# Memsets between all GpSimd record scatters and first row gathers, one set of head sums moved to VectorE, and the surplus table built in the second expert

## The chip, the cores and the metric

The kernel runs on one core of a Trainium2 chip. The metric is the device time of one execution in microseconds (us). A core has the engines TensorE (PE, with its weight loads shown as PEld), VectorE (DVE), ScalarE (ACT), GpSimd (POOL) and SyncE (SP); SP and POOL issue the DMAs, and each engine works through its own instruction list in order.

## The reference, cut to what matters

```python
def _attn_ref(q, k, v):                      # 8 batches, 8 heads, 576 rows, 64 wide
    k_p = k.reshape(B, H, Sp, 8, D).mean(axis=3)      # keys and values pooled by 8: 72 of them
    v_p = v.reshape(B, H, Sp, 8, D).mean(axis=3)
    attn = softmax(q @ k_p.T / sqrt(D))
    return attn @ v_p

def _moe_ref(x, w_gate, w_noise, noise, w1, w2):      # x: 4608 tokens x 512, 8 experts
    noisy = x @ w_gate + log1p(exp(x @ w_noise)) * noise
    top2 = two largest of noisy per token; top2_w = softmax of the two
    for e in range(8):
        h = relu(x[mask_e] @ w1[e])                   # 512 -> 1024
        out[mask_e] += top2_w * (h @ w2[e])           # 1024 -> 512
```

Attention makes x; a router picks two of eight experts per token; each expert computes only its own tokens.

## The kernel before, in words

**Attention and routing.** Four pairs of batches follow each other, nine chunks of 128 tokens a pair. For each chunk TensorE makes scores, transposed weights and the output; ScalarE takes the exponentials; VectorE takes maxima, divides, and writes `x` (to DRAM) and per-head router sums `lg`. At the end of a pair `route` (a generator that is advanced piece by piece between chunks) adds the eight heads' sums up (lines 512 and 513, the head sums: on GpSimd for the first two pairs, on VectorE for the last two), finds the top two experts, and ranks each token within its expert by TensorE prefix sums. Each token's record (token, weight, where to send the result) is then written to its place in `rec_dram` by an indirect DMA of GpSimd: 18 scatters a pair, 128 records each (`scatter`, line 642). While attention runs, a memset of a spare tile `spacer` (line 649) stands between one scatter and the next; once it is over (`attending[0] = False`), none does.

**What hangs on the scatters.** GpSimd's list is one chain. After the second pair's 18 scatters it loads the first expert's first records (line 692) and gathers their token rows, tiles `xg0` to `xg3` (line 719); then come the third pair's 18 scatters, a load, and `xg4`, `xg5`; then the fourth pair's 18 scatters, the record loads that SP issues, and `xg6` to `xg9`.

**The experts.** Expert 0 is computed in three groups of tiles (0 to 3, 4 and 5, 6 to 9), every other expert in three too. `stage1` multiplies by w1 (line 1031), `stage2` by w2 (line 1142; line 1108 in the last group of an expert). For expert 0 the rows of a group are transposed on TensorE (`rows_of`, line 769) in the middle of the group before: those of the second group between its second and third tile, those of the third group, `xg6` to `xg9`, after the first of the two tiles of the second group's `stage2`. TensorE works in order, so a row tile that is late there holds up everything behind it. All matmuls are in three passes of fp32r pieces; the weights' pieces are made by ScalarE and VectorE (lines 480 and 481).

**The surplus table** (lines 1212 to 1248) lists experts with more tokens than planned, from the final counts `cnt`. It is written last in the code, but the scheduler puts its VectorE instructions where `cnt` is ready, in the first expert's first group, and its two small DMAs on SP there.

Of the kernel before, what the change touches and what calls it, by code (L numbers as in the profile page):

```python
# [8 lines left out]
F32 = mybir.dt.float32  # L9
F32R = mybir.dt.float32r  # L10
BF16 = mybir.dt.bfloat16
I32 = mybir.dt.int32
AF = mybir.ActivationFunctionType
OP = mybir.AluOpType
AX = mybir.AxisListType.X
# [4 lines left out]
def kernel(  # L20
# [12 lines left out]
    nc = tc.nc  # L33
    B, H, S, D = q.shape
    NTOK, DM = out.shape
    E = moe_w_gate.shape[1]
    DF = moe_w1.shape[2]
    P = 128
# [7 lines left out]
    NP = B // 2  # L46
# [4 lines left out]
    CAP = 1216  # L51
    OV_T = -(-(NTOK - CAP) // P)
    ER = CAP + OV_T * P
# [18 lines left out]
    dp = ctx.enter_context(tc.tile_pool(name="scratch", bufs=1, space=bass.MemoryType.DRAM))  # L72
    rp = ctx.enter_context(tc.tile_pool(name="route", bufs=1))
# [3 lines left out]
    rec_dram = dp.tile([E * ER, RW], I32, name="rec_dram")  # L77
# [4 lines left out]
    prow = cp.tile([P, 1], F32, name="prow")  # L82
# [407 lines left out]

    scq = []
    pace = [None]
    tail_rec = [None]
    attending = [True]
    spacer = ap_.tile([P, DM], F32, name="spacer")

    def route(pr, c0, c1, lg, psum):
        n = c1 - c0
# [8 lines left out]
        V = nc.vector  # L507
        L = t(NCH, 2 * E)
        for a, b in ((c0, c1 - 1), (c1 - 1, c1)):
            eng = nc.gpsimd if pr < NP // 2 else V  # L510
            for h in (4, 2):
                eng.tensor_add(lg[:, a:b, :h], lg[:, a:b, :h], lg[:, a:b, h:2 * h])
            eng.tensor_add(L[:, a - c0:b - c0], lg[:, a:b, 0], lg[:, a:b, 1])
            if b < c1:
                yield
                if pr < NP - 1:
                    yield
# [120 lines left out]
        V.tensor_add(word(2), later, tb)  # L638

        def scatter(c, i):  # L640
            def put():
                return nc.gpsimd.indirect_dma_start(  # L642
                    out=rec_dram[:, :],
                    out_offset=bass.IndirectOffsetOnAxis(ap=pos[:, i, c:c + 1], axis=0),
                    in_=rec[:, c, i, :], in_offset=None)

            if attending[0] and tail_rec[0] is not None:
                with tc.issue_after(tail_rec[0].ins), tc.issue_after(pace[0].ins):
                    gap = nc.gpsimd.memset(spacer, 0.0)
                with tc.issue_after(gap.ins):  # L650
                    s = put()
            else:
                s = put()
            tail_rec[0] = s
            tc.declare_no_dep(s.ins, group="rec_scatter", reason="distinct rows")
            if pr >= NP // 2:
                tc.declare_no_dep(s.ins, group="rec_load0", reason="rows of the other half")
            if pr == NP - 1:
                tc.declare_no_dep(s.ins, group="rec_load1", reason="rows of the other pairs")
            tc.add_to_no_dep_group("rec_scatter", s.ins)  # L660
            tc.add_manual_dep(s.ins, pace[0].ins.name,
                              mybir.DependencyInfo(mybir.DependencyClass.Sync, mybir.DependencyReason.DATA),
                              reason="paced")
# [52 lines left out]
    def gather(e, t):  # L716
        xg = wp.tile([P, DM], F32, tag="xg", name=f"xg{e}_{t}", bufs=4)
        if e == 0:
            g = nc.gpsimd.indirect_dma_start(
                out=xg, out_offset=None, in_=x_dram[:XT0 if t < 4 else NTOK, :],  # L720
                in_offset=bass.IndirectOffsetOnAxis(ap=xi[e, t], axis=0))
            if t < 4:
                tc.declare_no_dep(g.ins, group="xw1", reason="rows of the other half")
                tc.add_to_no_dep_group("xg0", g.ins)
        else:
            nr = 2 if t == 9 else 4
            row = pools[0].tile([P, DM], F32, tag="row", name=f"row{e}_{t}", bufs=4)
            turn_of("pool", lambda: nc.gpsimd.indirect_dma_start(  # L728
                out=row[:32 * nr], out_offset=None, in_=x_dram[:, :],
                in_offset=bass.IndirectOffsetOnAxis(ap=xi[e, t][:32 * nr], axis=0)))  # L730
            via = dp.tile([P, DM], F32, tag="via", name=f"via{e}_{t}", bufs=4)
            for r in range(nr):
                turn_of("sp", lambda: nc.sync.dma_start(
                    via.rearrange("(u j) (r c) -> j r u c", u=4, r=4)[:, r],
                    row[32 * r:32 * r + 32].rearrange("j (u c) -> j u c", u=4)))
            back.append(lambda: turn_of("sp", lambda: nc.sync.dma_start(xg[:, :nr * P], via[:, :nr * P])))
        XG[e, t] = xg
# [207 lines left out]
            gens.append(route(pr, 0, 5, lgs[pr], one))  # L945
    due.pop()()
    advance(100, 0)
    attending[0] = False
    ctx2.close()


# [37 lines left out]
    def count(e):  # L989
        rows[e] = nc.values_load(cnti[0:1, e:e + 1], engines=[mybir.EngineType.PE], min_val=0, max_val=NTOK)  # L990
# [179 lines left out]
    def hook1(i, f):  # L1170
        if i == 0 and f == 0:
            with tc.issue_after(s0[0].ins), tc.issue_after(s0[1].ins):
                next(rt, None)
        elif i == 0:
            next(rt, None)
            next(rt, None)
        advance(0, POPS[i][f])
# [10 lines left out]
                nc.gpsimd.drain()  # L1188

    NG = 3  # L1190
    for i, g in enumerate(groups):
        e = g[0]
        if i % NG == 1 and e + 1 < E:
            wgens += [weights(e + 1, 0), weights(e + 1, 1)]
        if joined(g):
            with tc.issue_after(lastmm[0].ins):
                count(e)
        stage1(g, (lambda f: hook1(i, f)) if i < 2 else flush if i == len(groups) - 1 else None)
        if i > 1:
            if i + 1 < len(groups):  # L1200
                with tc.issue_after(HT[g][-1][2].ins):
                    split(groups[i + 1])
        if i % NG:
            wadvance(100)
        if i % NG == NG - 1 and e + 1 < E:
            wgens += [weights(e + 1, 2), weights(e + 1, 3)]
        stage2(g, (lambda t, mm: hook(i, t, mm)) if i < 2 else None,
               groups[i + 2] if 0 < i < len(groups) - 2 else None)


    thr = rp.tile([P, OV_T], F32, name="thr")
    nc.gpsimd.iota(thr, pattern=[[P, OV_T]], base=CAP, channel_multiplier=0,
                   allow_small_or_imprecise_dtypes=True)
    NJ = E
    cj = cnt
    gt = rp.tile([P, E, OV_T], F32, name="gt")
    nc.vector.tensor_tensor(gt, cj.unsqueeze(2).to_broadcast([P, E, OV_T]),
                            thr.unsqueeze(1).to_broadcast([P, E, OV_T]), op=OP.is_gt)
    nt_ = rp.tile([P, NJ], F32, name="nt")
    nc.vector.tensor_reduce(out=nt_, in_=gt, axis=AX, op=OP.add)  # L1220
    cum = rp.tile([P, NJ], F32, name="cum")
    nc.vector.tensor_copy(cum[:, 0:1], nt_[:, 0:1])
    for j in range(1, NJ):
        nc.vector.tensor_add(cum[:, j:j + 1], cum[:, j - 1:j], nt_[:, j:j + 1])
    le = rp.tile([P, NJ], F32, name="le")
    nc.vector.tensor_scalar(le, cum, prow, None, op0=OP.is_le)
    ln_ = rp.tile([P, NJ], F32, name="ln")
    nc.vector.tensor_mul(ln_, le, nt_)
    red = rp.tile([P, 2], F32, name="red")
    nc.vector.tensor_reduce(out=red[:, 0:1], in_=le, axis=AX, op=OP.add)  # L1230
    nc.vector.tensor_reduce(out=red[:, 1:2], in_=ln_, axis=AX, op=OP.add)
    sg = rp.tile([P, 2], F32, name="sg")
    nc.vector.tensor_sub(sg[:, 1:2], prow, red[:, 1:2])
    nc.vector.tensor_scalar(sg[:, 0:1], red[:, 0:1], float(ER), float(CAP), op0=OP.mult, op1=OP.add)
    nc.vector.scalar_tensor_tensor(sg[:, 0:1], sg[:, 1:2], float(P), sg[:, 0:1], op0=OP.mult, op1=OP.add)
    NTAB = 64
    nc.vector.scalar_tensor_tensor(sg[:, 1:2], red[:, 0:1], -float(CAP), sg[:, 0:1], op0=OP.mult, op1=OP.add)
    nc.vector.tensor_single_scalar(sg[:, 1:2], sg[:, 1:2], float(P + (E - 1) * CAP), op=OP.add)
    tab = rp.tile([P, 3], I32, name="tab")
    nc.vector.tensor_copy(tab[:, 2:3], sg[:, 1:2])  # L1240
    nc.vector.tensor_copy(tab[:, 0:1], sg[:, 0:1])
    nc.vector.tensor_copy(tab[:, 1:2], red[:, 0:1])
    tot = rp.tile([P, 1], I32, name="tot")
    nc.vector.tensor_copy(tot, cum[:, NJ - 1:NJ])
    tab_dram = dp.tile([NTAB, 3], I32, name="tab_dram")
    nc.sync.dma_start(tab_dram[:, :], tab[:NTAB])
    tabr = rp.tile([1, 3 * NTAB], I32, name="tabr")
    nc.sync.dma_start(tabr, tab_dram.rearrange("(o a) c -> o (a c)", o=1))
    totr = nc.values_load(tot[0:1, 0:1], min_val=0, max_val=NTAB)
    mctx.close()  # L1250
    op = ctx.enter_context(tc.tile_pool(name="over", bufs=1))
# [78 lines left out]
```

## Time and profile before

| | us |
|---|---|
| median of three runs | 1018.15 (1017.35 to 1019.13) |
| the profiled execution's own time | 1028.72 |
| its span, first to last instruction | 1026.9 |
| TensorE busy | 995.0 (97%) |
| VectorE busy | 549.2 (53%) |
| GpSimd busy | 402.7 (39%) |
| granted TensorE clock, mean | 0.981 |

Attention takes roughly the first 195 us, the experts the rest. The busy share of TensorE says little, since matmuls overlap; what counts are the places where it waits or runs at a lower granted clock (1.0 is 2.4 GHz, 0.5 is 1.2 GHz). A line such as "PE bank L1031 <- issue" means that TensorE stood idle before an instruction of line 1031 and that the profile names nothing that it waited for.

### The profile page before, as it was taken

What the parts mean: (1) busy time and instruction counts of PE and PEld (TensorE: products, weight loads), DVE (VectorE), ACT (ScalarE), POOL (GpSimd) and SP (SyncE); (2) the same over time, 40 slices, a digit from 0 to 9 for tenths busy, and PEclk for the clock granted to TensorE, in tenths of its full rate; (3) what the DMA queues carried; (4) which work ended last, traced back from release to release, by engine and by line L of the source; (5) the groups of instructions that cost most, each with busy time, mean ns of one, the idle gap of its engine ahead of it and who ended that gap; (6) DMA issues with size and microseconds to landing.
All of it is one profiled execution on the core that took longest, in us unless ns stands there. A gap on an engine that the chain in (4) does not pass through costs nothing.

```text
span 1026.9 us, 16502 instructions
## 1 busy us (share of the span) xinstructions
PE 995.0 (97%) x5832; PEld 891.8 (87%) x5832; DVE 549.2 (53%) x1277; ACT 344.8 (34%) x857; POOL 402.7 (39%) x470
## 2 busy tenths in 40 slices
PE   7999899898999999999999999999999999999996
PEld 6798887787998889898988898989888988898995
DVE  5799688781344454644464446344644455456341
ACT  4787587540213222421142124211421232123120
POOL 4025777956300442145115421452154216422514
PEclk8999899998999999999999999999999999999999
DMA  9997953462707765677268636772687357744623
GB/s 275 339 309 220 292 171 108 131 186 58 205 3 229 206 185 155 192 238 208 69 186 256 206 111 203 249 214 68 188 242 233 105 172 235 251 147 135 213 87 133
DMA packets 137382, 190.36 MB, mean 185 GB/s; under 512 B 29155, under 2 KB 84084, under 8 KB 137274
## 3 DMA queue, kind: packets, MB, share of 16 engines
q1 hardware_dynamic: 111834, 121.84, 39.2%
q0 software_dynamic: 25440, 67.05, 21.2%
q8 instruction: 72, 1.18, 0.5%
q14 instruction: 36, 0.29, 0.1%
HBM read 126.07 MB, written 70.74 MB: 192 GB/s over the span
## 4 chain that ended last, share of the span: by engine, by line
PE 89%; POOL 3%; issue 3%; ACT 2%; DVE 1%; DMA 1%; SPq 0%; POOLq 0%; ACTq 0%; DVEq 0%
PE bank L1031 38%; PE bank L1142 28%; PE bank L1108 10%; PE a L408 4%; PE s L375 3%; PE ep L393 2%; PE qp L347 2%; POOL rec_dram L642 1%; ACT ex L382 1%; ACT eT L395 1%; POOL out_dram L1087 1%; ACT kbd L302 0%; DVE k L233 0%; PE vr L325 0%; PE kT L298 0%
## 5 line engine op out<-in xcount | busy, mean ns | idle before, releaser
L1031 PE MATMUL bank<-xh,w 128*128 128x512 f32 (+6 forms) x1536 | 393.3, 340 | 2.3 <-issue 2.3
L1031 PEld LDWEIGHTS bank<-xh,w 128*128 128x128 f32 x1536 | 272.8, 190 | 24.3 <-issue 3.9
L1142 PE MATMUL bank<-w,hh 128*128 128x512 f32 x880 | 271.3, 389 | 0.0
L1031 PE MATMUL bank<-xl,w 128*128 128x512 f32 (+6 forms) x768 | 261.4, 340 | 2.4 <-issue 2.0
L1042 ACT ACTIVATE hh<-bank 128x512 fp32r<-128x512 f32 (+4 forms) x192 | 97.0, 509 | 469.4 <-PE bank L1031 365.7
L1043 DVE SCALAR_TENSOR_TENSOR hl<-bank,hh 128x512 fp32r<-128x512 f32 (+4 forms) x192 | 110.6, 580 | 244.9 <-ACT hh L1042 221.2
L1142 PEld LDWEIGHTS bank<-w,hh 128*128 128x128 f32 x880 | 164.9, 188 | 33.8
L1142 PE MATMUL bank<-w,hl 128*128 128x512 f32 x440 | 171.3, 389 | 0.0
L1031 PEld LDWEIGHTS bank<-xl,w 128*128 128x128 f32 x768 | 145.9, 190 | 12.7 <-issue 1.8
L1083 POOL DMA_DIRECT2D slot_dram<-yt x17 | 9.8, 576 | 269.0 <-DVE yt L1079 218.5
L1079 DVE SCALAR_TENSOR_TENSOR pv<-bank,raw,pv 128x128 f32<-128x128 f32 x196 | 55.6, 344 | 111.5 <-DMA pv<-slot_dram,raw 51.7
L1108 PE MATMUL bank<-hh,w 128*128 128x240 f32 (+3 forms) x512 | 103.5, 297 | 0.5 <-issue 0.4
L642 POOL DMA_INDIRECT rec_dram<-rec,pos x72 | 80.9, 1124 | 42.4 <-DVE rd L415 18.6
L1142 PEld LDWEIGHTS bank<-w,hl 128*128 128x128 f32 x440 | 82.6, 188 | 17.2
L1063 POOL DMA_INDIRECT pv<-slot_dram,raw x70 | 68.8, 983 | 64.2 <-DMA slot_dram<-ys 32.8
L481 DVE TENSOR_TENSOR w<-wst,w 128x512 fp32r<-128x512 f32 x128 | 82.7, 683 | 9.4 <-ACT w L480 9.1
L1108 PEld LDWEIGHTS bank<-hh,w 128*128 128x128 f32 x512 | 82.7, 189 | 1.4 <-issue 1.4
L1083 POOL DMA_DIRECT2D slot_dram<-pv x55 | 31.8, 578 | 126.5 <-DVE pv L1079 92.2
L480 ACT CAST w<-wst 128x512 fp32r<-128x512 f32 x128 | 72.9, 619 | 24.6 <-DMA wst<-in_moe_w_dram 24.5
L728 POOL DMA_INDIRECT row<-x_dram,raw x70 | 72.2, 1031 | 21.3 <-issue 20.1
L1108 PE MATMUL bank<-hl,w 128*128 128x320 f32 (+3 forms) x256 | 76.2, 297 | 0.4 <-issue 0.4
L382 ACT ACTIVATE ex<-s,mx 128x72 f32<-128x72 f32 x288 | 70.8, 343 | 8.9 <-DVE mx L380 8.4
(166 smaller groups left out, 1058.6 us busy)
## 6 DMA issues: line engine op xcount, KB each, us to landing
wst<-in_moe_w_dram SPq DMA_DIRECT2D x64, 512.0 KB
via<-row SPq DMA_DIRECT2D x266, 64.0 KB
xg<-via SPq DMA_DIRECT2D x63, 256.0 KB
slot_dram<-pv POOLq DMA_DIRECT2D x55, 256.0 KB
k<-in_k_dram SPq DMA_DIRECT2D x7, 1280.0 KB
v<-in_v_dram SPq DMA_DIRECT2D x16, 512.0 KB
x_dram<-xr SPq DMA_DIRECT2D x16, 512.0 KB
q<-in_q_dram SPq DMA_DIRECT2D x7, 1024.0 KB
```

The lines of the kernel that those rows point to most:

```text
L382: lasta[0] = nc.scalar.activation(ex[:, jj, EPOS[h] * G:(EPOS[h] + 1) * G], sv[:, i], AF.Exp, bias=mx[:, i:i + 1])
L480: nc.scalar.copy(hv, sv)
L481: nc.vector.tensor_sub(lv, sv, hv.bitcast(F32))
L642: return nc.gpsimd.indirect_dma_start(out=rec_dram[:, :], out_offset=bass.IndirectOffsetOnAxis(ap=pos[:, i, c:c + 1], axis=0), in_=rec[:, ...
L728: turn_of("pool", lambda: nc.gpsimd.indirect_dma_start(out=row[:32 * nr], out_offset=None, in_=x_dram[:, :], in_offset=bass.IndirectOffset ...
L1031: nc.tensor.matmul(part(ph), w1s(e, a, db, f), part(xs[b][:, db]), start=(i == 0), stop=(i == 3 * NDB - 1))
L1042: act = nc.scalar.activation(hh[:, :n], ph[:, :n], AF.Relu)
L1043: last = nc.vector.scalar_tensor_tensor(hl[:, :n], ph[:, :n], 0.0, hh[:, :n].bitcast(F32), op0=OP.max, op1=OP.subtract)
L1063: turn_of("pool", lambda: nc.gpsimd.indirect_dma_start(out=pv[:np_], out_offset=None, in_=slot_dram[:P + e * CAP, :], in_offset=bass.Indir ...
L1079: nc.vector.scalar_tensor_tensor(r_, y_, wc, pv[:plain] if plain else r_, op0=OP.mult, op1=OP.add)
L1108: nc.tensor.matmul(part(py), w2s(e, b, f)[:, mb * P:(mb + 1) * P], part(hs[f][a]), start=(i == 0), stop=(i == 3 * NFB - 1))
L1142: mm = nc.tensor.matmul(py, hs[f][a][:, cs], w2s(e, b, f), start=(i == 0), stop=(i == 3 * NFB - 1))
```

## The change

There are three edits. `spaced` puts the memset between any two of the record scatters, and also between the ten gathers of expert 0's rows and their neighbours, in and after attention alike; after attention it clears a part of the last pair's `lg` tile, since `spacer` is gone by then. The head sums of the second pair move from GpSimd to VectorE. The surplus table's code becomes a function that is called before the second expert's second group, tied by `issue_after` to that point.

```diff
-    tail_rec = [None]
-    attending = [True]
-    spacer = ap_.tile([P, DM], F32, name="spacer")
+    tail_ind = [None]
+    spacer = [ap_.tile([P, DM], F32, name="spacer")]
+
+    def spaced(make):
+        if tail_ind[0] is None:
+            tail_ind[0] = make()
+        else:
+            with tc.issue_after(tail_ind[0].ins):
+                gap = nc.gpsimd.memset(spacer[0], 0.0)
+            with tc.issue_after(gap.ins):
+                tail_ind[0] = make()
+        return tail_ind[0]
...
-            eng = nc.gpsimd if pr < NP // 2 else V
+            eng = V if pr else nc.gpsimd
...
-            if attending[0] and tail_rec[0] is not None:
-                with tc.issue_after(tail_rec[0].ins), tc.issue_after(pace[0].ins):
-                    gap = nc.gpsimd.memset(spacer, 0.0)
-                with tc.issue_after(gap.ins):
-                    s = put()
-            else:
-                s = put()
-            tail_rec[0] = s
+            s = spaced(lambda: nc.gpsimd.indirect_dma_start(
+                out=rec_dram[:, :],
+                out_offset=bass.IndirectOffsetOnAxis(ap=pos[:, i, c:c + 1], axis=0),
+                in_=rec[:, c, i, :], in_offset=None))
...
-            g = nc.gpsimd.indirect_dma_start(
+            g = spaced(lambda: nc.gpsimd.indirect_dma_start(
                 out=xg, out_offset=None, in_=x_dram[:XT0 if t < 4 else NTOK, :],
-                in_offset=bass.IndirectOffsetOnAxis(ap=xi[e, t], axis=0))
+                in_offset=bass.IndirectOffsetOnAxis(ap=xi[e, t], axis=0)))
...
-    attending[0] = False
+    spacer[0] = lgs[NP - 1][:, :4].rearrange("p j h c -> p (j h c)")
...
+        if i == NG + 1:
+            with tc.issue_after(pace[0].ins):
+                tot, tabr = over_table()
```

On GpSimd, where attention ends (`rec` are the records, `raw` the loaded ones, `xg` the gathered rows), the list before reads:

```order
L642 DMA rec_dram<-rec_0_2328,pos_0_2471 37376x4 x2
L692 DMA raw_4_2841<-rec_dram 128x8
L719 DMA xg_4_2843<-x_dram,raw_4_2841 128x512
L719 DMA xg_5_2845<-x_dram,raw_4_2841 128x512
L642 DMA rec_dram<-rec_0_2901,pos_0_2979 37376x4 x14
L1083 DMA slot_dram<-pv_2812 128x512
L642 DMA rec_dram<-rec_0_2901,pos_0_2979 37376x4 x4
```

and now:

```order
L650 DMA rec_dram<-rec_0_2332,pos_0_2475 37376x4
L501 MEMSET lg_2171 128x512
L691 DMA raw_4_2847<-rec_dram 128x8
L718 DMA xg_4_2849<-x_dram,raw_4_2847 128x512
L501 MEMSET lg_2171 128x512
L718 DMA xg_5_2852<-x_dram,raw_4_2847 128x512
L501 MEMSET lg_2171 128x512
L650 DMA rec_dram<-rec_0_2909,pos_0_2987 37376x4
L501 MEMSET lg_2171 128x512
L650 DMA rec_dram<-rec_0_2909,pos_0_2987 37376x4
L501 MEMSET lg_2171 128x512
```

The runs of 14 and 4 scatters have become single ones with a memset after each, and the gathers too.

On VectorE at the end of the second pair (`mx` are maxima that the exponentials wait for, `rt` the router's tiles), the list before reads:

```order
L380 TENSOR_REDUCE mx_4_1_0_1494<-s_4_1_0_1490 128x6
L414 TENSOR_SCALAR rd_3_1_1_1520<-a_3_1_1_1513 128x8
L233 TENSOR_TENSOR v_197<-v_197 112x6x128
L415 RECIPROCAL rd_3_1_1_1520<-rd_3_1_1_1520 128x8
L380 TENSOR_REDUCE mx_4_1_1_1537<-s_4_1_1_1533 128x6
L419 TENSOR_TENSOR xr_3_1_0_1469<-a_3_1_1_1513,rd_3_1_1_1520 128x512
L421 TENSOR_TENSOR lg_835<-a_3_1_1_1513,rd_3_1_1_1520 128x128
L239 TENSOR_TENSOR vs_1546<-v_197 112x384
L380 TENSOR_REDUCE mx_4_1_2_1574<-s_4_1_2_1571 128x4
L520 SCALAR_TENSOR_TENSOR rt_0_2_1561<-rt_0_1_1484 128x72
```

and now:

```order
L380 TENSOR_REDUCE mx_4_1_0_1494<-s_4_1_0_1490 128x6
L521 TENSOR_TENSOR lg_835<-lg_835 128x8x64
L414 TENSOR_SCALAR rd_3_1_1_1520<-a_3_1_1_1513 128x8
L521 TENSOR_TENSOR lg_835<-lg_835 128x8x32
L415 RECIPROCAL rd_3_1_1_1520<-rd_3_1_1_1520 128x8
L522 TENSOR_TENSOR rt_0_1_1484<-lg_835 128x128
L419 TENSOR_TENSOR xr_3_1_0_1469<-a_3_1_1_1513,rd_3_1_1_1520 128x512
L421 TENSOR_TENSOR lg_835<-a_3_1_1_1513,rd_3_1_1_1520 128x128
L380 TENSOR_REDUCE mx_4_1_1_1537<-s_4_1_1_1533 128x6
L521 TENSOR_TENSOR lg_835<-lg_835 128x64
```

Six head-sum instructions have moved in from GpSimd, and the first instruction that reads their result (line 520 before) stands further down.

## Rows read from the trace of the kernel before

**Rows 1.** The page: busy time, share of the span, instructions of each engine.

```profile
PE 995.0 (97%) x5832; PEld 891.8 (87%) x5832; DVE 549.2 (53%) x1277; ACT 344.8 (34%) x857; POOL 402.7 (39%) x470
```

**Rows 2.** Waits of TensorE: line, releaser, us in total, times, longest.

```profile
PE bank L1031 <- issue: 4.4, 7, 1.1
PE ep L393 <- ACT ex L382: 3.0, 1, 3.0
```

**Rows 3.** Timeline of TensorE: start, us, instruction, idle before and its releaser.

```profile
242.85 0.40 PE L1031 MATMUL bank<-xh,w 128*128 128x256 f32 x2 [1.12 <-issue]
```

**Rows 4.** Windows: PE, PEld, DVE, ACT, POOL busy (instructions), granted clock, DMA, GB/s.

```profile
240.40:248.60 8.20, 3.83 (x16) 2.41 (x14) 1.13 (x4) 0.00 (x0) 5.37 (x7) 0.70 0.19 65
248.60:254.00 5.40, 5.40 (x25) 5.40 (x26) 0.85 (x2) 0.84 (x3) 2.42 (x3) 0.50 0.57 76
254.00:261.00 7.00, 7.00 (x61) 7.00 (x60) 3.14 (x9) 1.85 (x5) 3.64 (x5) 1.00 0.57 187
```

**Rows 5.** Chain that ended last, around the third group's transposes: start, us, what.

```profile
261.15 5.47 PE bank L1142 x24
266.62 1.92 PE bank L769 x16
268.54 5.49 PE bank L1142 x24
```

**Rows 6.** Timeline of VectorE at the second pair's end.

```profile
114.18 0.23 DVE L520 SCALAR_TENSOR_TENSOR rt<-rt 128x72 f32<-128x72 f32 x1 [4.51 <-POOL rt L513]
```

**Rows 7.** Windows there, columns as in rows 4.

```profile
112.00:115.10 3.10, 0.13 (x2) 0.00 (x0) 0.92 (x4) 0.62 (x3) 1.92 (x5) 0.83 1.04 277
115.10:124.20 9.10, 9.09 (x52) 8.58 (x53) 6.79 (x24) 4.83 (x17) 6.39 (x7) 0.50 0.74 255
```

**Rows 8.** Head sums: second pair on POOL, third on DVE (xcount | busy, mean ns).

```profile
L512 POOL TENSOR_TENSOR lg<-lg 128x512 f32<-128x512 f32 (+3 forms) x4 | 2.6, 640 | 0.2
L513 POOL TENSOR_TENSOR rt<-lg 128x128 f32<-128x128 f32 (+1 forms) x2 | 0.7, 337 | 0.2
...
L512 DVE TENSOR_TENSOR lg<-lg 128x512 f32<-128x512 f32 (+3 forms) x4 | 1.5, 372 | 0.0
L513 DVE TENSOR_TENSOR rt<-lg 128x128 f32<-128x128 f32 (+1 forms) x2 | 0.5, 234 | 0.0
```

**Rows 9.** Timeline of POOL: a gather, spaced scatters, scatters without a memset.

```profile
178.54 0.96 POOL L719 DMA_INDIRECT xg<-x_dram,raw  x1 [0.30 <-issue]
179.80 1.22 POOL L642 DMA_INDIRECT rec_dram<-rec,pos  x1 [0.30 <-issue]
...
199.18 0.98 POOL L642 DMA_INDIRECT rec_dram<-rec,pos  x1 [0.16 <-issue]
200.86 0.98 POOL L642 DMA_INDIRECT rec_dram<-rec,pos  x1 [0.17 <-DVE rt L543]
...
242.89 0.97 POOL L642 DMA_INDIRECT rec_dram<-rec,pos  x1 [0.30 <-issue]
244.17 0.97 POOL L642 DMA_INDIRECT rec_dram<-rec,pos  x1 [0.30 <-issue]
```

**Rows 10.** Timeline of POOL: the second record load.

```profile
215.36 0.58 POOL L692 DMA_DIRECT2D raw<-rec_dram  x1 [4.39 <-DMA rec_dram<-rec,pos]
```

**Rows 11.** Timeline of POOL and SP: last gather of expert 0, first of expert 1.

```profile
254.81 0.95 POOL L719 DMA_INDIRECT xg<-x_dram,raw  x1 [0.30 <-issue]
259.91 1.01 POOL L728 DMA_INDIRECT row<-x_dram,raw  x1 [0.30 <-issue]
...
263.41 8.12 SPq L733 DMA_DIRECT2D via<-row  x16
```

**Rows 12.** Lines of VectorE: 180 to 206, 300 to 400, and 209 to 227 us.

```profile
L481 DVE TENSOR_TENSOR w<-wst,w 128x512 fp32r<-128x512 f32 x5 | 3.4, 684 | 0.0
...
L481 DVE TENSOR_TENSOR w<-wst,w 128x512 fp32r<-128x512 f32 x16 | 10.3, 684 | 7.9 <-ACT w L480 7.9
...
L1224 DVE TENSOR_TENSOR cum<-cum,nt 128x1 f32<-128x1 f32 x7 | 1.1, 157 | 0.1
```

More of the change, by code (lines that the diff above doesn't have):

```diff
@@ L640, in scatter @@
         def scatter(c, i):
[L641 to L645, printed above, removed]
-            if attending[0] and tail_rec[0] is not None:
-                with tc.issue_after(tail_rec[0].ins), tc.issue_after(pace[0].ins):
-                    gap = nc.gpsimd.memset(spacer, 0.0)
-                with tc.issue_after(gap.ins):
-                    s = put()
-            else:
-                s = put()
-            tail_rec[0] = s
+            s = spaced(lambda: nc.gpsimd.indirect_dma_start(
+                out=rec_dram[:, :],
+                out_offset=bass.IndirectOffsetOnAxis(ap=pos[:, i, c:c + 1], axis=0),
+                in_=rec[:, c, i, :], in_offset=None))
             tc.declare_no_dep(s.ins, group="rec_scatter", reason="distinct rows")
@@ L1190, with over_table @@
     NG = 3
+    NTAB = 64
+    def over_table():
+        thr = rp.tile([P, OV_T], F32, name="thr")
+        nc.gpsimd.iota(thr, pattern=[[P, OV_T]], base=CAP, channel_multiplier=0,
+                       allow_small_or_imprecise_dtypes=True)
+        NJ = E
+        cj = cnt
+        gt = rp.tile([P, E, OV_T], F32, name="gt")
+        nc.vector.tensor_tensor(gt, cj.unsqueeze(2).to_broadcast([P, E, OV_T]),
+                                thr.unsqueeze(1).to_broadcast([P, E, OV_T]), op=OP.is_gt)
+        nt_ = rp.tile([P, NJ], F32, name="nt")
+        nc.vector.tensor_reduce(out=nt_, in_=gt, axis=AX, op=OP.add)
+        cum = rp.tile([P, NJ], F32, name="cum")
+        nc.vector.tensor_copy(cum[:, 0:1], nt_[:, 0:1])
+        for j in range(1, NJ):
+            nc.vector.tensor_add(cum[:, j:j + 1], cum[:, j - 1:j], nt_[:, j:j + 1])
+        le = rp.tile([P, NJ], F32, name="le")
+        nc.vector.tensor_scalar(le, cum, prow, None, op0=OP.is_le)
+        ln_ = rp.tile([P, NJ], F32, name="ln")
+        nc.vector.tensor_mul(ln_, le, nt_)
+        red = rp.tile([P, 2], F32, name="red")
+        nc.vector.tensor_reduce(out=red[:, 0:1], in_=le, axis=AX, op=OP.add)
+        nc.vector.tensor_reduce(out=red[:, 1:2], in_=ln_, axis=AX, op=OP.add)
+        sg = rp.tile([P, 2], F32, name="sg")
+        nc.vector.tensor_sub(sg[:, 1:2], prow, red[:, 1:2])
+        nc.vector.tensor_scalar(sg[:, 0:1], red[:, 0:1], float(ER), float(CAP), op0=OP.mult, op1=OP.add)
+        nc.vector.scalar_tensor_tensor(sg[:, 0:1], sg[:, 1:2], float(P), sg[:, 0:1], op0=OP.mult, op1=OP.add)
+        nc.vector.scalar_tensor_tensor(sg[:, 1:2], red[:, 0:1], -float(CAP), sg[:, 0:1], op0=OP.mult, op1=OP.add)
+        nc.vector.tensor_single_scalar(sg[:, 1:2], sg[:, 1:2], float(P + (E - 1) * CAP), op=OP.add)
+        tab = rp.tile([P, 3], I32, name="tab")
+        nc.vector.tensor_copy(tab[:, 2:3], sg[:, 1:2])
+        nc.vector.tensor_copy(tab[:, 0:1], sg[:, 0:1])
+        nc.vector.tensor_copy(tab[:, 1:2], red[:, 0:1])
+        tot = rp.tile([P, 1], I32, name="tot")
+        nc.vector.tensor_copy(tot, cum[:, NJ - 1:NJ])
+        tab_dram = dp.tile([NTAB, 3], I32, name="tab_dram")
+        nc.sync.dma_start(tab_dram[:, :], tab[:NTAB])
+        tabr = rp.tile([1, 3 * NTAB], I32, name="tabr")
+        nc.sync.dma_start(tabr, tab_dram.rearrange("(o a) c -> o (a c)", o=1))
+        return tot, tabr
@@ L1208 @@
                groups[i + 2] if 0 < i < len(groups) - 2 else None)
[L1211 to L1248, printed above, removed]
     totr = nc.values_load(tot[0:1, 0:1], min_val=0, max_val=NTAB)
```

## The prediction

> **What bounds the kernel now.** I read the page's busy times first, then the waits of TensorE, then windows and timelines round each wait. TensorE is busy for 97% of the span [rows 1], so the experts' matmuls set the time, and a change can act only where TensorE waits or runs at a lower clock. The list of waits leaves two large ones [rows 2]. One lies in attention, at the end of the second pair: 3.0 us for ScalarE's exponentials. The other lies at the start of the second group of expert 0: seven waits, 4.4 us together, for which the profile names nothing.
>
> The first: VectorE stands 4.51 us before line 520, because GpSimd's head sums are late [rows 6]. The maxima queued behind it hold up ScalarE, and that TensorE: 0.13 us busy in 3.1 us, then a granted clock of 0.50 for 9.1 us, in which it is busy all the time [rows 7].
>
> The second: from 240.4 to 261.0 us TensorE does the 96 matmuls of 256 columns. In the undisturbed last 7.0 us it does 61, or 0.115 us each [rows 4]; all 96 would take 11.0 us and took 20.6. For 8.2 us it issues one here and one there [rows 3], and then runs 5.4 us at 0.50 [rows 4]. Meanwhile GpSimd issues scatters without a memset, every 1.28 us [rows 9].
>
> Which of this is there when no profile is taken? The profiled execution took 1028.72 us, its span 1026.9 and 1.8 around it; the median is 1018.15, or 10.6 less. Without the second stall TensorE would reach the transposes of `xg6` to `xg9` at 240.4 + 11.0 + 5.5 = 256.9 instead of 266.6 [rows 5]. The last of these gathers is issued at 254.81; a like gather, issued at 259.91, lets SP start on its rows at 263.41, 3.5 us later [rows 11], so `xg9` is there at some 258.3. With 0.5 us for its own transposes (a quarter of 1.92, rows 5) the next matmuls would start at 258.8 instead of 268.54: 9.7 us saved of the 10.6 that are missing. The stall is also of single matmuls that wait for nothing. So I take it for a cost of recording, absent from the timed runs. Then GpSimd's chain of scatters and gathers is what TensorE waits for there, by 1.4 us (258.3 less 256.9), and it has no slack.
>
> **The memsets.** A scatter with a memset after it takes 1.68 us to the next (199.18 to 200.86), without one 1.28; a gather takes 1.26 to its neighbour [rows 9]. Each added memset therefore costs 0.4 to 0.42 us of GpSimd's chain. On the way to `xg9` are added:
> - four behind `xg0` to `xg3`: 1.7;
> - three at the third pair's last two scatters: 1.0, as the last lies under the 4.39 us in which the load waits for the scatters to land [rows 10];
> - two at `xg4` and `xg5`: 0.8;
> - seventeen between the fourth pair's 18 scatters: 7.0;
> - four at `xg6` to `xg9`, of which the first lies under the record load: 1.2.
>
> That is 11.7 us. From the second pair's first scatter on the chain is one engine's list, so nothing takes them up. `xg9` comes at 270.0 instead of 258.3. Queued behind its transposes on TensorE is the whole rest of the experts, so the 11.7 us reach the end. Bounds: 0, should the chain have as much slack in timed runs as the profile shows (258.3 against 266.6, less than the shift, so then 3.4 us stay), and 11.7.
>
> TensorE now idles some 13 us instead of 1.4. After the 3.0 us idle in attention 9.1 us ran at half clock [rows 7], a loss of 4.6. Here it is 0 if the timed runs already fall to 0.50 at this point, and 4.6 if only the longer wait does that; I take 2.0, since part of the slow stretch is the transposes that come in one by one.
>
> By the Trainium skill (SBUF — State Buffer, section "SBUF: two separate sides"), a GpSimd instruction can hold a port pair that VectorE shares and block it for a whole instruction, so each memset could also lengthen VectorE's work. The trace does not show that: the weight splits take 684 ns amid spaced scatters and 684 ns far from any [rows 12]. By the page the sum would be higher by up to 0.5 us a memset; I add nothing.
>
> **The head sums.** GpSimd's 3.3 us go and VectorE gets 2.0 (1.5 and 0.5, the third pair's price) [rows 8]. The wait before line 520 goes, with it TensorE's 3.0 us and the 9.1 us at half clock, 4.55 us of work: 7.5. Of VectorE's 2.0, which is busy 6.79 of 9.1 us there [rows 7], I let half reach TensorE: 6.5 us gained. The bounds are 7.5, and 1.0 if the 2.0 count in full and some other wait takes the clock down. The second pair's records are ready that much earlier, and so GpSimd's chain too: the gain holds for both. Late next there are VectorE's own maxima.
>
> **The surplus table.** Some 25 small VectorE instructions of about 0.16 us [rows 12], 4 us, leave the first group, where TensorE does not wait, and enter the second expert, where VectorE has 7.9 us idle before the weight splits alone [rows 12]. SP gets the two table DMAs there, in front of weight loads that are due much later. I put 0; if the cover were gone it would be 4 us.
>
> **Sum.** On the profile's own account: the third group's transposes end at 270.5 less 6.5 instead of 268.54, a loss of 4.6 to the clock follows, so the profiled time stays near 1029 (1028.7 + 2.0 − 6.5 + 4.6 = 1028.8), the gap having changed its place from 240 to 257. In timed runs, which I hold to be free of the first gap, it is 1018.15 + 11.7 + 2.0 − 6.5 = 1025.4 us, 0.7% slower.
>
> **Rivals.**
> - *The stall at 240 us is real and the memsets cure it.* For it speaks that it coincides with unspaced scatters, while spaced ones at 180 to 206 us go with no such line in the waits. Against it, the 10.6 us that timed runs lack and that no other gap of the profile could supply. Then TensorE gains 9.7 us and loses them at the transposes: 1018.15 + 2.0 + 4.6 − 6.5 = 1018.3, no change. It decides if timed runs hold the whole 268.54; without a fall of the clock it is 1013.7, faster.
> - *The stall is real and stays.* TensorE arrives 266.6 less 6.5, rows 3.4 us later: 1018.15 + 2.0 − 6.5 = 1013.7, or 1018.3 with the clock's fall; 1016 between. Scatters still come every 1.68 us, but half as much work sits between them.
> - *The chain has slack in timed runs* (GpSimd's instructions being shorter unrecorded), so that only the head sums count: 1018.15 − 6.5 = 1011.7. Against it, the 9.7 of 10.6 us above.
>
> **How the numbers follow.** The forecast has 0.50, a cured stall 0.27, a lasting one 0.13, the slack 0.10. The forecast's own range goes from 1018.15 + 11.7 − 7.5 = 1022.4 to 1018.15 + 11.7 + 4.6 − 1.0 = 1033.5, where the last two bounds seldom meet; I end it at 1031. The rivals go down to 1011.7; leaving out most of the last and the lowest of the others gives 1013.5 to 1031. A change of 0.2%, 2 us, is about what a measurement of this kernel can tell from none. Faster: 0.01 + 0.10 + 0.08 + 0.09 = 0.28. Same: 0.02 + 0.08 + 0.02 + 0.01 = 0.13. Slower: 0.47 + 0.09 + 0.03 + 0 = 0.59.
>
> **What the profile after would show.** If I am right, scatters of the last pair stand 1.68 us apart, `xg9`'s gather is issued about 5 us later than before (254.81 + 11.7 − 6.5), TensorE waits about 13 us before the transposes of `xg6` to `xg9` with a gather's DMA as releaser, the clock falls there, the seven waits without a releaser are gone, and the profiled time lies close to the timed one. Line 520's wait of 4.51 us is gone and the clock stays at 1.0 round 114 us. I am wrong if TensorE does not wait at these transposes, if the gap of profiled to timed stays at 10 us, or if a new wait in attention takes the 6.5.

## The result and the profile after

The changed kernel takes 1029.28 us in the median of 5 runs (1025.14 to 1030.06), the kernel before 1018.15 (1017.35 to 1019.13, 5 runs): a ratio of 1.0101, 95% interval 1.008 to 1.0122. It is slower by some 11 us; 1025.4 was forecast. The profiled execution took 1030.06 us, its span 1028.1, mean granted clock 0.983.

The first row answers [rows 1]: the page's busy times. GpSimd has grown by 12.4 us, the added memsets less the head sums, and VectorE by 2.4, about the head sums; TensorE's 97% say as little as before.

```profile
PE 994.1 (97%) x5832; PEld 890.1 (87%) x5832; DVE 551.6 (54%) x1283; ACT 345.0 (34%) x857; POOL 415.1 (40%) x494
```

Next the waits of TensorE, largest first, against [rows 2]. The seven waits without a releaser at 240 us are gone and so is the 3.0 us behind ScalarE. In their place stand rows of expert 0 that have not landed (9.2 us in six waits). One wait without a releaser remains, 2.0 us at line 1107.

```profile
PE bank L768 <- DMA xg<-x_dram,raw: 9.2, 6, 3.7
...
PE bank L1107 <- issue: 2.0, 1, 2.0
PE bank L1030 <- DVE pv L1080: 1.5, 1, 1.5
```

The timeline of TensorE shows where: before the transposes of `xg4` and `xg5` (221.36, 223.03) and of `xg6` to `xg9`. Between the two sets a bank of the matmuls waits for VectorE's `pv`, and VectorE for a store of `pv` to `slot_dram`, which GpSimd issues from the same list as scatters and memsets.

```profile
221.36 1.13 PE L768 MATMUL bank<-ident,xg 128*128 128x128 f32 x4 [2.81 <-DMA xg<-x_dram,raw]
223.03 1.13 PE L768 MATMUL bank<-ident,xg 128*128 128x128 f32 x4 [0.54 <-DMA xg<-x_dram,raw]
...
248.39 0.39 PE L1030 MATMUL bank<-xh,w 128*128 128x256 f32 x1 [1.52 <-DVE pv L1080]
...
259.26 1.13 PE L768 MATMUL bank<-ident,xg 128*128 128x128 f32 x4 [3.71 <-DMA xg<-x_dram,raw]
...
264.75 1.13 PE L768 MATMUL bank<-ident,xg 128*128 128x128 f32 x4 [1.16 <-DMA xg<-x_dram,raw]
...
398.47 0.78 PE L1107 MATMUL bank<-hh,w 128*128 128x240 f32 x2 [1.99 <-issue]
```

The last row is the wait without a releaser, in the second expert's last group. A granted clock of 0.50 for 3.4 us stands behind it. e9 below has such a wait of 2.74 us there; the other recordings have none over 1.1 us at this line. No run here shows what causes it.

Windows of TensorE alone (busy, instructions, granted clock, DMA share, GB/s), against [rows 4, 7]: the clock now stays at 1.00 through 112 to 124 us, and it falls behind both sets of waits instead.

```profile
112.00:124.00 12.00, 12.00 (x112) 1.00 1.08 343
218.50:228.00 9.50, 6.16 (x19) 0.64 0.21 59
240.40:248.60 8.20, 6.68 (x55) 1.00 0.10 33
255.50:268.70 13.20, 7.39 (x25) 0.61 0.72 181
```

GpSimd's timeline, against [rows 9, 11]: the fourth pair's scatters stand 1.67 to 1.68 us apart, and `xg9` is issued at 260.74 instead of 254.81.

```profile
231.49 0.97 POOL L650 DMA_INDIRECT rec_dram<-rec,pos  x1 [0.16 <-issue]
232.46 0.54 POOL L501 MEMSET lg<- 128x512 f32 x1
233.16 0.97 POOL L650 DMA_INDIRECT rec_dram<-rec,pos  x1 [0.17 <-issue]
...
260.74 0.96 POOL L718 DMA_INDIRECT xg<-x_dram,raw  x1 [0.16 <-issue]
```

VectorE's line 520 (529 here) no longer waits, against [rows 6]:

```profile
113.51 0.23 DVE L529 SCALAR_TENSOR_TENSOR rt<-rt 128x72 f32<-128x72 f32 x1
```

And the chain that ended last runs, in the second expert, through the surplus table: its write to DRAM (5.69 us until it has landed), then a weight load, a cast, two splits and `pv`, before TensorE goes on after a wait of 0.57 us. Nothing of this was foreseen.

```profile
349.76 5.69 DMA tab_dram<-tab
...
355.82 4.03 DMA wst<-in_moe_w_dram
...
360.53 1.29 DVE w L481 x2
...
364.30 2.35 PE bank L1030 x12
```

### The profile page after: what moved, and what is told of

It is laid out like the page before. It is cut to its first block, busy times and chain, and to the rows that moved or that the text cites. A ratio compares the mean times of both kernels' runs of the same rounds, so it can differ in the third digit from the quotient of the medians.

```text
span 1028.1 us, 16525 instructions
## 1 busy us (share of the span) xinstructions
PE 994.1 (97%) x5832; PEld 890.1 (87%) x5832; DVE 551.6 (54%) x1283; ACT 345.0 (34%) x857; POOL 415.1 (40%) x494
## 4 chain that ended last, share of the span: by engine, by line
PE 79%; DMA 6%; DVE 5%; POOL 4%; issue 3%; ACT 2%; SPq 1%; POOLq 0%; DVEq 0%; ACTq 0%
PE bank L1030 32%; PE bank L1141 23%; PE bank L1107 10%; PE a L408 5%; PE s L375 3%; PE ep L393 2%; DMA wst<-in_moe_w_dram 2%; PE qp L347 1%; POOL rec_dram L650 1%; DVE w L481 1%; POOL lg L501 1%; DMA v<-in_v_dram 1%; ACT ex L382 1%; POOL out_dram L1086 1%; DMA tab_dram<-tab 1%
## 5 line engine op out<-in xcount | busy, mean ns | idle before, releaser
L1030 PEld LDWEIGHTS bank<-xl,w 128*128 128x128 f32 x768 | 144.6, 188 | 10.3
L1107 PEld LDWEIGHTS bank<-hh,w 128*128 128x128 f32 x512 | 83.9, 192 | 2.2 <-issue 2.2
```

What stands on the lines that cost most here:

```text
L1030: nc.tensor.matmul(part(ph), w1s(e, a, db, f), part(xs[b][:, db]), start=(i == 0), stop=(i == 3 * NDB - 1))
L1107: nc.tensor.matmul(part(py), w2s(e, b, f)[:, mb * P:(mb + 1) * P], part(hs[f][a]), start=(i == 0), stop=(i == 3 * NFB - 1))
```

## The experiments

All ratios are to the kernel before, with 95% intervals. The kernels of one round shared its runs, so kernels of different rounds are best compared by their ratios. The theory at the start was that of the prediction: the stall at 240 us belongs to the recording, GpSimd's chain to `xg9` has no slack in timed runs, so each memset on it costs its 0.4 us and the clock some 2 us more.

**The first round: parts alone.** All four are edits of the kernel before. e2 is the change's `spaced` with its calls at scatters and gathers and nothing else; e3 is e1 with the change's `over_table`; e1 and e4 are one line each:

```diff
e1, line 510
-            eng = nc.gpsimd if pr < NP // 2 else V
+            eng = V if pr else nc.gpsimd
e4, line 494
-    attending = [True]
+    attending = [False]
```

> The second pair's head sums on VectorE, and nothing else of the change. My theory: 6.5 us less than before (bounds 1.0 to 7.5), so 1011.7; the wait of 4.51 us before line 520 and the half clock round 114 us are gone, and GpSimd's chain to xg9 moves forward by as much. In the profile the stall at 240 us stays, and the profiled time again lies some 10 us above the timed one. Rival, that half a chain's gain is lost behind GpSimd: the scatters of the second pair start no earlier, xg9 comes at the same time, and the gain is under 2 us.

Measured: 1015.03 us, 0.9972 (0.9953 to 0.999). A gain, but of 2.9 us and not 6.5. Line 520's wait and the slow clock went as expected; the profile has no stall at 240 us and takes 1013.66, amid the timed runs, both against what I had expected.

> The added memsets alone: head sums and surplus table stay as before. My theory (the recorded stall is absent in timed runs, the chain to xg9 has no slack): 1018.15 + 11.7 + 2.0 = 1031.9; TensorE waits for the gathers of xg4 to xg9, and the profiled time lies within 2 us of the timed one. Rival, the stall is real and cured: 9.7 us less on one side and about as much lost at the transposes, so 1018 to 1025. Rival, the chain has slack: 1018.

Measured: 1031.09 us, 1.0137 (1.0117 to 1.0157), 13.9 us of 1018.15 where 13.7 were expected. The memsets alone are the loss; as expected, TensorE waits for the gathers of `xg4` to `xg9` (8.7 us), and the profiled run takes 1030.03.

> The changed kernel with the added memsets taken out again: head sums on VectorE and the surplus table in the second expert. My theory: the table costs 0, so the same time as with the head sums alone, 1011.7, and some 13.7 us less than the changed kernel was forecast to take. Rival, the table's VectorE work is felt: up to 4 us more than the head sums alone.

Measured: 1016.99 us, 0.9998 (0.9976 to 1.002), so 0.26% above e1: the table looked as if it cost 2.6 us, on the rival's side, though the two intervals overlap.

> The kernel before without any memset between scatters, those of the second and third pair's scatters taken out too. My theory (unspaced scatters cost TensorE nothing in timed runs; each memset lengthens GpSimd's chain by 0.4): the chain to xg9 is earlier by up to 13 us, the wait of 1.4 us before the transposes and its share of the clock go, so 1015 to 1017; in the profile stalls of single matmuls without a releaser appear during the second and third pair's scatters too, and the profiled time lies 20 us or more above the timed one. Rival, the stall is real: it comes in attention too, 8 to 10 us for each pair's scatters, and the timed runs are 10 to 20 us slower than before.

Measured: 1006.48 us, 0.9897 (0.9878 to 0.9917): faster than I had expected, and the profiled run took 1005.49. My second half was plainly wrong: no scatter is spaced in this kernel, and its recording has no stall anywhere. TensorE waits for no gather. In attention the wait at line 520 has nearly gone too, with the head sums still on GpSimd, since they are reached earlier there. The timelines of GpSimd (the sums) and of VectorE (what waited for them), against [rows 6]:

```profile
105.99 2.66 POOL L512 TENSOR_TENSOR lg<-lg 128x512 f32<-128x512 f32 x2 [0.34 <-DVE lg L421]
```
```profile
110.77 0.23 DVE L520 SCALAR_TENSOR_TENSOR rt<-rt 128x72 f32<-128x72 f32 x1 [0.47 <-POOL rt L513]
```

**The second round: the stall, the table, the slack.** e5 is the kernel before, unedited. e6 is e4 with the edit of e1. e7 is e4 with `over_table` called in the second expert. e8 is e4 with a memset only between the fourth pair's scatters:

```diff
-            if attending[0] and tail_rec[0] is not None:
+            if pr == NP - 1 and tail4[0]:
...
+            tail4[0] = pr == NP - 1
```

> The kernel before, unchanged, recorded once more. If the stall of single matmuls at 240 us is the price of recording unspaced scatters, as the prediction had it, this profile shows it again and takes some 10 us more than 1018. Rival, which the three profiles of e1, e3 and e4 speak for (unspaced scatters in all, no such stall in any, each profiled time within its kernel's timed ones): it was an event of that one execution, and this profile takes 1016 to 1022 without it.

Measured: 1016.34 us, no stall. In the stretch of [rows 4] TensorE is busy all the time; the transposes of `xg6` to `xg9` run through without a wait; what it waits for is `xg5`, 2.21 us, with a loss of clock behind it. First the windows (columns as above), then the timeline of TensorE, then that of GpSimd, against [rows 11].

```profile
112.00:124.00 12.00, 9.96 (x57) 0.57 0.80 258
222.80:235.00 12.20, 9.99 (x40) 0.86 0.10 24
240.40:248.60 8.20, 8.20 (x71) 1.00 0.25 45
```
```profile
225.04 0.75 PE L769 MATMUL bank<-ident,xg 128*128 128x128 f32 x4 [2.21 <-DMA xg<-x_dram,raw]
...
255.13 2.08 PE L769 MATMUL bank<-ident,xg 128*128 128x128 f32 x16
```
```profile
251.79 0.95 POOL L719 DMA_INDIRECT xg<-x_dram,raw  x1 [0.31 <-issue]
```

So the stall was an event of one execution. Eight recordings here (e1, e3 to e7, e11, e12) have no memset between the fourth pair's scatters, as the kernel before has none, and none of them shows it.

> No memset anywhere, and the second pair's head sums on VectorE. In e4 the wait at line 520 is down to 0.47 us with the head sums on GpSimd, and TensorE waits for no gather. My theory: the head sums were late because of GpSimd's memsets ahead of them, so that moving them is worth only what is left, 0 to 1 us; 1005.5 to 1007.5, the same as e4. Rival, GpSimd's slower sums themselves cost TensorE: 3 us or more less than e4.

Measured: 1006.92 us, 0.9876 (0.9844 to 0.9909); the interval overlaps that of e4. Without memsets the place of the head sums decides nothing that can be told.

> No memset anywhere, and the surplus table in the second expert; against e4 it is the table alone. The prediction had 0. e3 against e1 gave 0.26% more with it. If that is the table, this kernel takes 2 to 4 us more than e4, 1008.5 to 1010.5, and its profile has a wait in the second expert that e4 has not; if it was the gathers' waits and the clock round them, 1006.5.

Measured: 1009.55 us, 0.9906 (0.9869 to 0.9942); the time alone overlaps e4's, the profile does not. SP issues the table's write, one weight load (`wst`), and then stands in front of the table's read from 331.18 to 335.34; the next weight loads follow at 335.69. In e4 they went out at 330.38. e3 and the changed kernel show the same hold (to 343.76 and to 355.47). First SP's timeline of e7, then that of e4.

```profile
329.57 0.51 SPq L1229 DMA_DIRECT2D tab_dram<-tab  x1
330.33 0.37 SPq L736 DMA_DIRECT2D xg<-via  x1
330.75 0.43 SPq L459 DMA_DIRECT2D wst<-in_moe_w_dram  x1
335.34 0.25 SPq L1231 DMA_DIRECT2D tabr<-tab_dram  x1
335.69 3.80 SPq L459 DMA_DIRECT2D wst<-in_moe_w_dram  x3
```
```profile
329.92 0.36 SPq L736 DMA_DIRECT2D xg<-via  x1
330.38 10.02 SPq L459 DMA_DIRECT2D wst<-in_moe_w_dram  x4
```

Some 10 us later TensorE of e7 pays: a wait of 1.78 us, then a stretch at a lower clock (0.69 over 5.5 us, a loss of 1.7).

```profile
344.73 0.44 PE L1031 MATMUL bank<-xh,w 128*128 128x384 f32 x1 [1.78 <-DVE pv L1079]
```
```profile
344.50:350.00 5.50, 5.27 (x19) 0.69 0.24 92
```

> No memset in attention and at the gathers, but the 17 between the fourth pair's scatters as in the changed kernel. In e4 the last gather is issued at 236.34, its rows are there some 3.5 us later, and TensorE's last four transposes of xg are at 246.7, so GpSimd's chain has some 6.8 us of slack there; 17 times 0.41 is 7.0. My theory: the scatters stand 1.68 apart, xg9 is issued 7 us later, TensorE waits 0 to 1 us, and the time is that of e4, 1006 to 1009. Rival, a memset costs TensorE by itself, through VectorE's work or otherwise: 17 of the change's memsets at 13/31 us each, some 7 us more than e4, 1013.5.

Measured: 1007.85 us, 0.9893 (0.9857 to 0.9928), which cannot be told from e4's time. From `xg5` to `xg9` GpSimd takes 41.4 us (200.85 to 242.27) and took 33.7 in e4 (202.68 to 236.34): the 7.0 us are there (7.8 measured), and TensorE waits 0.64 us. The 7 us more that the rival asked for would be 1013.5, beyond the interval (up to 1011.1). So these memsets cost nothing that can be told where the chain has slack.

**The third round: dose, place, and the two causes.** e9 and e10 are edits of the changed kernel, e11 of the kernel before, e12 of e7.

```diff
e9, in spaced (tail2 is set where spacer is exchanged)
+            if tail2[0]:
+                with tc.issue_after(gap.ins):
+                    gap = nc.gpsimd.memset(spacer[0], 0.0)
e10, in gather
-            g = spaced(lambda: nc.gpsimd.indirect_dma_start(
+            g = (lambda f: f())(lambda: nc.gpsimd.indirect_dma_start(
e11, in scatter
-            if attending[0] and tail_rec[0] is not None:
+            if pr and attending[0] and tail_rec[0] is not None:
e12, out of over_table and behind the experts' loop
+    nc.sync.dma_start(tab_dram[:, :], tab[:NTAB])
+    nc.sync.dma_start(tabr, tab_dram.rearrange("(o a) c -> o (a c)", o=1))
```

> The changed kernel with a second memset behind each one that is issued after attention: the third pair's last two scatters, xg4 and xg5, the fourth pair's 18 scatters, xg6 to xg9. Some 25 of them lie on GpSimd's chain and each takes 0.54 us. My theory: scatters 2.22 us apart, xg9 13.5 us later than in the changed kernel (274), TensorE waits for all of it, so 1029.3 + 13.5 = 1043, up to 1046 with the clock. Rival, part of the change's cost is the clock's fall alone, which is already paid: the same 13.5 at the least of it, but no more than 1041; rival, the wait is set by the scatters' landing and not by their issue: under 1035.

Measured: 1042.3 us, 1.0235 (1.0215 to 1.0255). `xg9` came at 271.39, not 274, because attention ended earlier in this recording; counted from the third pair's last scatter it is 13.6 us more, where 13.5 were expected. One wait before the transposes takes nearly all of it, 16.15 us against 3.71 in the changed kernel:

```profile
267.67 1.13 PE L772 MATMUL bank<-ident,xg 128*128 128x128 f32 x4 [16.15 <-DMA xg<-x_dram,raw]
```

> The changed kernel without the memsets at the ten row gathers; those between all scatters stay. By the steps of the prediction these are worth 1.7 at xg0 to xg3, 0.8 at xg4 and xg5 and 1.2 at xg6 to xg9: 3.7 us off GpSimd's chain, and 1025.6 us, down to 1023 if a fall of the clock goes with them. Rival, the first four lie in slack (attention's transposes come later anyway): 2 us, 1027.3.

Measured: 1023.07 us, 1.0069 (1.0049 to 1.009). That is under the changed kernel by 6.2 us in the medians but by 3.3 in the ratios, whose intervals overlap; 3.7 stood in the sum. In the recordings `xg9` is issued 6.0 us earlier (254.71 against 260.74), but 2.9 of these stand already at the second pair's last scatter (162.84 against 165.78), ahead of every memset that was taken out. So 3.1 us are the edit's. The stretches at a clock of 0.50 are shorter (3.4 and 6.8 us against 6.9 and 10.2); whether that is worth anything beyond the 3.7 cannot be told.

> The kernel before without the 17 memsets between the first pair's scatters; the head sums stay on GpSimd. My theory: the wait of 4.51 us at line 520 was GpSimd's queue, so it falls to 0.5 us as in e4, the clock stays at 1.0 round 114 us, the second pair's scatters start 4 to 6 us earlier, and the time falls as far as the chain does: 1012.5 to 1015.5, as with the head sums moved or a little better. Rival, GpSimd's slower sums themselves are what VectorE waits for: the wait stays above 2 us and the time at 1017 to 1018.

Measured: 1012.64 us, 0.995 (0.9931 to 0.9968), as expected. The second pair's scatters start 3.5 us earlier than in e5 (132.31 against 135.81), a little under the 4 to 6 expected. The wait at line 520 is 0.47 us:

```profile
113.17 0.23 DVE L520 SCALAR_TENSOR_TENSOR rt<-rt 128x72 f32<-128x72 f32 x1 [0.47 <-POOL rt L513]
```

So the head sums were late because GpSimd reached them late, not because it is slow at them.

> As e7 (no memset, the surplus table computed in the second expert), but the table's two DMAs are issued after the experts' loop. In e7 the read of the table stands on SP from 330.75 to 335.34 us behind its own write, and four weight loads behind it; TensorE then waits 1.78 us at 343 us and the clock falls. My theory: that wait goes, no other comes, and the time is that of e4 and e6, 1005.5 to 1007.5. Rival, the table's 25 VectorE instructions are what makes VectorE late: the wait stays, 1008.5 to 1010.

Measured: 1006.24 us, 0.9891 (0.9872 to 0.991). The wait of 1.78 us is gone with the table's VectorE work still in place (at 308 to 312 us). The interval overlaps e7's, so it is the profile that tells, not the time. The scheduler left the write where it was; the read now comes behind all four weight loads:

```profile
330.55 1.46 SPq L1255 DMA_DIRECT2D tab_dram<-tab  x1
337.84 2.04 SPq L459 DMA_DIRECT2D wst<-in_moe_w_dram  x2
339.97 0.28 SPq L1256 DMA_DIRECT2D tabr<-tab_dram  x1
```

The times, by what GpSimd takes from the third pair's last scatter to `xg9` and by when it issues `xg9`, read from each timeline (the kernel before by e5's recording; medians in its rounds 1018.3 to 1018.5):

| kernel | stretch, us | `xg9` issued at, us | median, us |
|---|---|---|---|
| e4, no memset | 42.8 | 236.3 | 1006.5 |
| before | 43.5 | 251.8 | 1018.3 |
| e11, first pair free | 44.3 | 249.1 | 1012.6 |
| e1, head sums alone | 45.1 | 249.6 | 1015.0 |
| e8, fourth pair's memsets alone | 50.2 | 242.3 | 1007.9 |
| e10, none at the gathers | 50.4 | 254.7 | 1023.1 |
| e2, memsets alone | 51.5 | 264.0 | 1031.1 |
| changed kernel | 51.7 | 260.7 | 1029.3 |
| e9, doubled | 65.3 | 271.4 | 1042.3 |

From the changed kernel to e9, 13.6 us more on the chain are 13.0 us more of time. From e4 to e8, 7.4 us more are 1.4, within their intervals: these two begin the stretch at 193.5 and 192.0, the kernel before at 208.3, so their chain is early. The length of the stretch alone does not order the times; when `xg9` is issued does, for all nine. Each place is read from one recording, and two kernels that are not in the table lie above this order, e3 (248.7 and 1017.0 us) and e7 (236.0 and 1009.6), both with the table's read in front of weight loads, as the changed kernel, e9 and e10 have it.

## Why the prediction was right, and where it was not

**The direction and the size: right, by the memsets.** 11.7 + 2.0 us forecast, 13.9 measured with the memsets alone (11.9 to 16.0 by e2's interval). The price of one was right: from the third pair's last scatter to `xg9` the changed kernel takes 8.2 us more than e5, where 9.0 of the 11.7 belong there (0.8 + 7.0 + 1.2). Over the whole chain, from the second pair's last scatter to `xg9`, e2 takes 95.6 us (168.38 to 263.99) and e5 83.9 (167.87 to 251.79): 11.7 more, as summed. A second set added 13.6 us, where 13.5 were expected.

**"I take it for a cost of recording": wrong.** The timed runs fit a kernel that is free of the stall, but so is another recording of the same program (e5, 1016.34 us). It was one execution's event, and the 10.6 us between profiled and timed went with it. My test of it, that the two times lie close together after the change, was met and proved nothing, since e1, e3 and e4 meet it with unspaced scatters. What halted TensorE in that execution is open.

**"By 1.4 us" and "it has no slack": right in effect, wrong in place.** The kernel before does wait for the chain, but at `xg5` (2.2 us, with 3.4 us at a clock of 0.50 behind it). At `xg6` to `xg9` e5's rows land, by the 3.5 us of [rows 11], at 251.8 + 3.5 = 255.3, and TensorE needs the last near 255.1 + 1.5 = 256.6, so there is slack of 1.3 us there and not a wait of 1.4. That the chain has no slack was worked out from a recording with a stall that no other has; that it held, at another place, was in part luck. The change's time is lost in two places, at `xg4` and `xg5` (3.4 us of waits) and at `xg6` to `xg9` (5.8), and not in one wait of 13 us.

**The head sums, −6.5: the step that was mis-sized.** e1 gives −2.9 (−4.8 to −1.0). Line 520's wait, TensorE's 3.0 us and the slow clock went, as forecast. "The gain holds for both" did not: the second pair's scatters start 3.8 us earlier than in e5 (132.04 against 135.81), each right behind VectorE's last `rec` write, and `xg4` only 2.0 (215.48 against 217.46), since in this recording the record load waits longer for the scatters to land. In e3, the other kernel with these sums moved and no memset added, `xg4` comes 3.5 us earlier than in e5; `xg9` comes 2.2 us earlier in e1 and 3.1 in e3. GpSimd's timeline of e1, then that of e5, against [rows 10]:

```profile
210.81 0.58 POOL L692 DMA_DIRECT2D raw<-rec_dram  x1 [5.35 <-DMA rec_dram<-rec,pos]
...
215.48 0.99 POOL L719 DMA_INDIRECT xg<-x_dram,raw  x1 [4.10 <-DMA wst<-in_moe_w_dram]
```
```profile
213.07 0.58 POOL L692 DMA_DIRECT2D raw<-rec_dram  x1 [3.77 <-DMA rec_dram<-rec,pos]
...
217.46 1.00 POOL L719 DMA_INDIRECT xg<-x_dram,raw  x1 [3.81 <-PE bank L1142]
```

TensorE, ahead by more, waits 5.0 us at `xg4` and `xg5`. Where GpSimd's chain sets the end, only what that chain gains counts. The 3.6 us between −6.5 and −2.9 are nearly all of the 3.9 between 1025.4 and 1029.28: 13.9 for the memsets less 2.9 for the head sums is 11.0 us, where the changed kernel lost 11.1 by the medians and 10.3 by the ratio.

**The clock, +2.0.** Forecast for one place and reached with another account. An estimate of what a fall cost is half of TensorE's busy time in the stretch at 0.50; it is one from above, since a transpose that only waits for the next row loses nothing by running slowly. The windows of these stretches (columns as above), first in the changed kernel behind its two sets of waits, then in e5:

```profile
220.90:227.80 6.90, 5.91 (x18) 0.51 0.15 41
258.50:268.70 10.20, 7.34 (x24) 0.50 0.69 203
```
```profile
113.50:123.70 10.20, 9.66 (x54) 0.50 0.78 260
226.10:229.50 3.40, 3.40 (x10) 0.50 0.05 6
```

The changed kernel loses (5.9 + 7.3) / 2 = 6.6 us there, and 1.7 more at 398 us (3.3 busy at 0.50); e5 loses (9.7 + 3.4) / 2 = 6.5, of which 4.8 at the head sums. So the 4.8 gained in attention are given back at the gathers. With the memsets alone (e2) it is 10.0 us, 3.5 more than in e5, where 2.0 were forecast.

**The surplus table, 0: wrong in what was counted.** Its VectorE work is hidden, as said. Its read of what SP has just written was costed as being "in front of weight loads that are due much later", and holds those loads for 4 us, until the write has landed; e7 and e12 show it. How much that is in the changed kernel was not measured apart: its own wait there is 0.57 us, e3 against e1 gives 2.6 with overlapping intervals, and the other two edits, 11.0 us together, leave nothing for it. Intervals of some 2 us do not decide between these.

**The port.** The prediction let each memset perhaps lengthen VectorE's work. By the Trainium skill (SBUF — State Buffer, section "SBUF: two separate sides"), a VectorE operation with two SBUF inputs contends only with a GpSimd operation that reads SBUF, and a memset (`lg<-`, no input) reads none. The trace agrees for the weight splits, which have two inputs (`w<-wst,w`): between 203 and 250 us they take the same time in e9 with two memsets in each gap and in e4 with none, so no run here shows a block. VectorE's lines grouped, first e9, then e4:

```profile
L481 DVE TENSOR_TENSOR w<-wst,w 128x512 fp32r<-128x512 f32 x6 | 3.8, 687 | 2.3 <-ACT w L480 2.3
```
```profile
L481 DVE TENSOR_TENSOR w<-wst,w 128x512 fp32r<-128x512 f32 x9 | 5.9, 688 | 2.5 <-ACT w L480 2.5
```

**A better version** came out: no memset at all (e4, e6, e12) runs in 1006.2 to 1006.9 us, 1.1% under the kernel before and 2.2% under the changed one.

## What to carry to other kernels

An instruction put between DMA issues costs nothing that can be told while the queue it sits in is ahead of its reader (e8), and all that it adds to the queue's period, with a fall of the clock on top, once it is not (e2, e9): work out the slack at each reader before pricing it. When one engine's chain sets the end, a gain at another engine's front is worth only what the chain gains, and the rest comes back as a new wait. A profiled execution that lies outside the timed runs should be recorded again before anything is built on its odd stretch.

## What the runs showed of the hardware that was not expected

- One execution in which TensorE shows 16 matmuls in 8.2 us [rows 4] with nothing named as the reason; e5, the same program, shows 71 there.
- A read of a 768-byte table behind its own write held SP's list, and the weight loads behind it, from 331.18 to 335.34 us in e7; in the changed kernel the write took 5.69 us to land.
- After a wait of 16.15 us the granted clock was 0.50 for 8 us from 267 us on and 0.64 over the next 7; after one of 1.52 us (changed kernel, 248.39) it stayed at 1.00. The length of a wait alone does not tell: behind 1.78 us in e7 the clock fell to 0.51 for 3.4 us, behind 1.97 us in e3 (before the transposes at 217.72) it stayed at 1.00.
